# V loads on ScalarE's DMA queue instead of SyncE's, in a one-token attention and SwiGLU kernel

## The chip, the cores and the metric

The kernel runs on one core of one Trainium2 chip. The metric is the device time of one execution in microseconds (us). A core has TensorE (PE in the profile; PEld are its weight loads), VectorE (DVE), ScalarE (ACT), GpSimd (POOL) and SyncE (SP). Each engine works through its own list of instructions in order; a DMA is issued by an instruction in such a list, and what it moves then goes on without the engine.

## The reference

One decoding step for a batch of 4 sequences, with 32 heads of 192, a window of 2048 positions out of the 8192 in the cache, a model width of 640 and an FFN width of 1536. All inputs are bf16.

```
xn  = layernorm(x)                                    # 4 x 640
q   = (xn @ wq) as 32 heads of 192
k, v = the last 2048 positions of k_cache, v_cache    # per batch and head
p   = softmax(q . k * 192**-0.5)
att = (p . v, heads joined: 6144) @ wo
ffn = (silu(xn @ w1) * (xn @ w3)) @ w2
out = x + att + ffn
```

K and V of the window are 32 heads x 4 sequences x 2048 x 192 x 2 bytes each, 100.7 MB for K and the same for V. The weights add 21.6 MB: wq and wo 7.9 MB each, w1, w3 and w2 2.0 MB each.

## The kernel before, in words

**Tiles.** For each head, K is one tile of 128 partitions x 64 positions x 192 (`kt`, 3 MB, two buffers), and V another (`vt`, 3 MB, three buffers). A partition belongs to one of the 4 sequences and holds 64 successive positions, so a row of a load is 24 KB in one piece. The three tiles of wq at the start use the three V buffers.

**Scores.** A head is cut into four units `u = 4h .. 4h+3`. `mult(u)` (L202) multiplies a quarter of K with the query, which is laid out on all partitions (`qbc`), on VectorE. `adder(u)` (L213) adds the product over the 192 columns down to 32 with six matmuls against the identity. `reduce_quarter(u)` (L221) adds those 32 on VectorE, which gives 16 scores for each partition.

**Softmax.** `chain_lmax` (L225) takes the maximum on each partition, `chain_tr` (L230) transposes it, `chain_gmax` (L235, L238) takes the maximum of each sequence, `chain_bc` (L243 to L249) spreads it back with a matmul and computes the exponential `ex` on ScalarE, and `chain_z` (L257) masks it by sequence.

**Values.** `pv(h)` (L265) multiplies `z` with V in 32 matmuls and ScalarE copies the result to `o_raw` (L268). `ge_tot`, `ge_norm` (L280), `ge_tr` (L290) and `ge_copy` (L299) transpose and normalise it. After every four heads `ge_proj` (L194, L195) multiplies with a piece of wo and adds to two accumulators in PSUM, which hold the sum of x, attention and FFN until the end.

**FFN.** Its parts are spread between the heads: w1 is loaded at head 6, w3 after it and w2 last, all in one buffer, so each load waits until the weight before it has been used.

**What sets the order.** There is no automatic scheduler. `add(slot, phase, function, ...)` enters each step in a table, and at the end the table is run through by slot, then phase, then order of entry; each engine gets its instructions in that order. Unit `u` has its product in slot `u`; head `h` has its first unit in `u0 = 4h` and its last in `ul = 4h + 3`. Head h's other steps stand some slots later.

**DMA queues.** All loads but x are issued by SyncE, in slot order:

```
add((h - KBUFS + 1) * GQ, 0, load_k, h)
add(u0 + (2 if h != H - 3 else 5), 0, load_v, h, 1 if h < H - 1 else 2)
```

K of head h is thus issued behind the last product of head h-2, which frees its buffer; V of head h is issued behind K of head h+1. V of head 29 stands at `u0 + 5`, three slots later than the others. The last V is loaded in two pieces. wo for a group of four heads, w1, w3 and w2 stand between them. In a program without a wait SyncE would run ahead of all: what holds it are the waits for buffers.

Of the kernel before, what the change touches and what calls it, by code (L numbers as in the profile page):

```python
# [10 lines left out]
FP32 = mybir.dt.float32  # L11
BF16 = mybir.dt.bfloat16
# [6 lines left out]
def kernel(  # L19
# [14 lines left out]
    KBUFS: int = 2,  # L34
    VBUFS: int = 3,
    PBUFS: int = 4,
    L: int = 8,
    FFN_HEAD: int = 6,
):
    nc = tc.nc  # L40
    P = 128
    B, Sq, D = A_x.shape
    _, H, Sk, Dh = A_k_cache.shape
# [3 lines left out]
    FC = F // P  # L47
    PB = P // B
    NJ = W // PB
    GQ = 4  # L50
# [7 lines left out]
    RPP = QW // P  # L58
    NU = H * GQ
# [4 lines left out]
    assert D % P == 0 and F % QC == 0 and P % B == 0 and W % (PB * GQ) == 0  # L64
    assert JQ * DD == 512 and JQ % 2 == 0 and 2 * Dh <= 512 and 0 < N1 <= 512
    assert (H * Dh) % QC == 0 and NQ % 6 == 0 and QW % P == 0 and Dh % RPP == 0 and P == HG * CT
    assert 2 * H * Dh <= NJ * Dh and KBUFS == 2 and VBUFS == 3

    ctx.enter_context(tc.manual_schedule())
    const = ctx.enter_context(tc.tile_pool(name="const", bufs=1))  # L70
    fpool = ctx.enter_context(tc.tile_pool(name="ffn", bufs=1))
# [4 lines left out]
    small = ctx.enter_context(tc.tile_pool(name="small", bufs=3))  # L76
# [9 lines left out]
    kts, vts, prs, pss, scs, exs, zs = {}, {}, {}, {}, {}, {}, {}  # L86
    wos, o_raws, rsums, rtbs, chs, ges, oTs = {}, {}, {}, {}, {}, {}, {}
# [7 lines left out]
    def load_v(h, pieces=1):  # L95
        vt = vpool.tile([P, NJ, Dh], BF16, tag="vt")
        src = v_win[:, h].rearrange("b (p j) d -> p b j d", p=PB)
        n = NJ // pieces
        for i in range(pieces):
            nc.sync.dma_start(out=vt[:, i * n:(i + 1) * n, :].rearrange("q j d -> q (j d)"),  # L100
                              in_=src[:, :, i * n:(i + 1) * n, :].rearrange("p b j d -> p b (j d)"))
        vts[h] = vt

# [3 lines left out]
        wos[hg] = wo_t  # L107

    x_sb = const.tile([B, D], BF16, name="x_sb")
    nc.scalar.dma_start(out=x_sb[:], in_=A_x.rearrange("b s d -> (b s) d"))  # L110
    wq_v = A_wq.rearrange("(p kc) n -> p kc n", kc=KC)
    wq_rows = []
    for k0 in range(0, KC, 2):
        n = min(2, KC - k0)
        wt = vpool.tile([P, 2, H * Dh], BF16, tag="vt")
        nc.sync.dma_start(out=wt[:, 0:n, :].rearrange("p k n -> p (k n)"),
                          in_=wq_v[:, k0:k0 + n, :].rearrange("p k n -> p (k n)"))
# [49 lines left out]
    for c0 in range(0, NQ, 6):  # L167
        qps = [pool.tile([P, QC], FP32, tag=tag, name="qps")
               for pool, tag in ((ps_add, "ps"), (ps_add, "ps"), (ps_o, "o_ps"), (ps_o, "o_ps"), (ps_m, "mt"), (ps_t, "t"))]
        for kc in range(KC):  # L170
            for i, qp in enumerate(qps):
                nc.tensor.matmul(qp[:], lhsT=xnT[:, kc].rearrange("p a b -> p (a b)"),  # L172
                                 rhs=wq_rows[kc][:, (c0 + i) * QC:(c0 + i + 1) * QC],
                                 start=(kc == 0), stop=(kc == KC - 1))
# [8 lines left out]
    o_banks = []  # L183
    for i in range(2):
        o_ps = ps_o.tile([P, 2 * Dh], FP32, tag="o_ps", name="o_ps")
# [7 lines left out]
    def acc_add(lhsT, rhs, first=False, last=False):  # L193
        nc.tensor.matmul(acc0[:], lhsT=lhsT, rhs=rhs[:, 0:N0], start=first, stop=last)  # L194
        nc.tensor.matmul(acc1[:], lhsT=lhsT, rhs=rhs[:, N0:D], start=first, stop=last)  # L195
# [62 lines left out]
                                in1=mask_b[:].unsqueeze(1).to_broadcast([P, NJ, B]), op=ALU.mult)  # L258
        zs[h] = z

    def pv(h):
        o_ps, z, vt = o_banks[h % 2], zs.pop(h), vts.pop(h)
        for jj in range(NJ // 2):
            c = jj % 4
            nc.tensor.matmul(o_ps[c * CT:c * CT + 2 * B, :], lhsT=z[:, 2 * jj:2 * jj + 2, :],  # L265
                             rhs=vt[:, 2 * jj:2 * jj + 2, :], start=(jj < 4), stop=(jj >= NJ // 2 - 4))
        o_raw = small.tile([P, 2, Dh], FP32, tag="o_raw", bufs=2, name="o_raw")
        nc.scalar.copy(out=o_raw[:].rearrange("q two d -> q (two d)"), in_=o_ps[:])  # L268
        o_raws[h] = o_raw


    def ge_tot(h):
# [35 lines left out]
    hT = const.tile([P, FC, B], BF16, name="hT")  # L308
    g_bf = const.tile([B, F], BF16, name="g_bf")
    ffn = {}  # L310
# [29 lines left out]

    w2_v = B_w2.rearrange("(p c) n -> p c n", c=FC)

    W2C = [(0, FC // 2), (FC // 2, FC - 2), (FC - 2, FC)]

    def w2_load(i):
        if i == 0:
            ffn["w2"] = fpool.tile([P, FC, D], BF16, tag="w", name="w2")
        c0, c1 = W2C[i]
        nc.sync.dma_start(out=ffn["w2"][:, c0:c1, :].rearrange("p c n -> p (c n)"),
                          in_=w2_v[:, c0:c1, :].rearrange("p c n -> p (c n)"))  # L350

    def ffn_out(i):
        for c in range(*W2C[i]):
            acc_add(hT[:, c, :], ffn["w2"][:, c, :], last=(c == FC - 1))

    sched = defaultdict(list)

    def add(slot, phase, fn, *args):
        sched[slot].append((phase, len(sched[slot]), fn, args))


    for h in range(H):
        u0, ul = h * GQ, h * GQ + GQ - 1
        last = h >= H - 2
        if h >= KBUFS:
            add((h - KBUFS + 1) * GQ, 0, load_k, h)
        add(u0 + (2 if h != H - 3 else 5), 0, load_v, h, 1 if h < H - 1 else 2)
        for u in range(u0, ul + 1):
            add(u, 1, mult, u)
            add(u + 1, 2, adder, u)  # L370
            add(u + 1, 8, reduce_quarter, u)
        add(ul + 1, 9, chain_lmax, h)
        add(ul + 2, 3, chain_tr, h)
        add(ul + 2, 4, chain_gmax, h)
        add(ul + 3, 3, chain_bc, h)
        add(ul + 3, 4, chain_z, h)
        add(ul + 4, 5, ge_tot, h)
        add(ul + 4, 9, ge_norm, h)
        add(u0 + L, 7, pv, h)
        add(u0 + L + (1 if h != H - 2 else 3), 7, ge_tr, h)  # L380
        add(u0 + L + (2 if h != H - 2 else 3), 9, ge_copy, h)
    for hg in range(NG):
        a = ((hg + 1) * HG - 1) * GQ + L + 3
        add(hg * HG * GQ + 8 if hg < NG - 1 else NU, 0, wo_load, hg)
        add(a, 6, ge_proj, hg, 0, RPP // 2)
        add(a + 1, 6, ge_proj, hg, RPP // 2, RPP)
    f = FFN_HEAD * GQ
    add(f, 0, ffn_load, "w1", B_w1)
    add(f + 7, 7, ffn_in, "w1", g_bf)
    add(f + 7, 7, ffn_silu)  # L390
    add(f + 7, 9, ffn_load, "w3", B_w3)
    add(f + 15, 7, ffn_up)
    add(f + 15, 8, ffn_h)
    add(f + 16, 7, ffn_transpose)
    add((H - 1) * GQ + 1, 0, w2_load, 0)
    add(NU, 0, w2_load, 1)
    add(NU, 0, w2_load, 2)
    add(NU + L - 5, 8, ffn_out, 0)
    add(NU + L + 2, 0, ffn_out, 1)
    add(NU + L + 2, 0, ffn_out, 2)  # L400

    for s in sorted(sched):
        for phase, _, fn, args in sorted(sched[s], key=lambda e: (e[0], e[1])):
            fn(*args)

    res = ppool.tile([B, D], BF16, tag="pr", name="res")
    nc.vector.tensor_copy(out=res[:, 0:N0], in_=acc0[:])
    nc.scalar.copy(out=res[:, N0:D], in_=acc1[:])
# [31 lines left out]
```

## Time and profile before

| | |
|---|---|
| time, median of 3 runs | 536.11 us (536.1 to 538.67) |
| the profiled execution, its own time | 536.1 us |
| its span, from first to last instruction | 534.3 us |
| granted clock of TensorE, mean | 0.885 |
| TensorE matmul, busy | 378.0 us (71%) |
| VectorE, busy | 353.5 us (66%) |
| ScalarE, busy | 50.3 us (9%) |
| bytes moved, mean rate | 223.39 MB, 418 GB/s |
| one K load, from issue to landing | 19.2 us (median) |
| one V load, from issue to landing | 26.6 us (median) |
| product of one unit (L202) | 1.75 us |
| reduction of one unit (L221) | 0.68 us |
| six matmuls of an adder (L213) | 1.46 us at full clock, 2.64 us where the clock stood near half |

The profile is of one execution. Its page has the busy time of each engine, the span in 40 equal slices of 13.4 us (with a DMA row: how busy the 16 DMA engines were, in tenths), the DMA queues, and the chain of work that ended last: what each step waited for, followed back from the last instruction. A time to landing runs from the issue to the moment when the last byte has arrived, so it includes the transfers that stand ahead in the queue. Idle time of an engine that isn't on that chain costs nothing.

### The profile page before, as it was taken

To read this page: it belongs to the slowest core of one execution; us is meant where nothing else is said; L and a number is where in the kernel's file an instruction comes from. 1 tells how busy PE (TensorE), PEld (TensorE's weight loads), DVE (VectorE), ACT (ScalarE), POOL (GpSimd) and SP (SyncE) were. 2 spreads that over 40 slices of the span, in tenths; PEclk is the share of its full clock that TensorE was granted. 3 is DMA by queue.
4 is the path that set the end of the run, shared out by engine and by line. 5 is a ranking of instruction groups with operands and counts; after the bars stand their busy time and mean duration, and the time that the engine had idled before them with its cause. 6 is when DMAs were issued, how large, how long until landed. Compare 5 with 4: busy or idle time off the path is not lost.

```text
span 534.3 us, 6753 instructions
## 1 busy us (share of the span) xinstructions
PE 378.0 (71%) x2948; PEld 184.1 (34%) x2949; DVE 353.5 (66%) x471; ACT 50.3 (9%) x150; POOL 1.1 (0%) x8
## 2 busy tenths in 40 slices
PE   2875886886666876678748768777648865587777
PEld 1322332443233343333313333333313433243244
DVE  3169785876356686785857767687756778586660
ACT  2111000000410200000000000000000000010010
POOL 0000000000000000000000000000000000000000
PEclk9879886899967999697978997799987999698798
DMA  8999999999999999999999999999999999999992
GB/s 359 436 436 393 420 437 437 427 430 431 433 434 431 428 438 423 434 434 428 432 433 431 432 429 432 436 424 432 432 434 432 428 429 437 431 432 392 429 398 81
DMA packets 11709, 223.39 MB, mean 418 GB/s; under 512 B 1304, under 2 KB 1312, under 8 KB 2720
## 3 DMA queue, kind: packets, MB, share of 16 engines
q1 hardware_dynamic: 11672, 222.96, 97.6%
q8 instruction: 23, 0.38, 0.3%
q14 instruction: 6, 0.05, 0.0%
q10 hardware_dynamic: 8, 0.01, 0.0%
HBM read 222.96 MB, written 0.01 MB: 417 GB/s over the span
## 4 chain that ended last, share of the span: by engine, by line
DMA 56%; PE 24%; DVE 16%; ACT 3%; issue 1%; SPq 0%
DMA kt<-in_A_k_cache_dram 49%; PE ps L213 12%; DVE pr L202 11%; PE gp L290 5%; DMA vt<-in_A_v_cache_dram 3%; DMA wt<-in_A_wq_dram 3%; DVE sc L221 2%; PE qps L172 2%; PE o_ps L265 2%; ACT ex L249 1%; DVE z L257 1%; PE mt L243 1%; PE gt L322 1%; PE acc_240 L195 1%; PE acc_239 L194 1%
## 5 line engine op out<-in xcount | busy, mean ns | idle before, releaser
L213 PE MATMUL ps<-pr,idb 128*128 128x512 bf16 x768 | 219.1, 429 | 133.7 <-DVE pr L202 133.7
L202 DVE TENSOR_TENSOR pr<-kt,qbc 128x3072 bf16<-128x3072 bf16 x128 | 223.6, 1747 | 91.5 <-DMA kt<-in_A_k_cache_dram 91.0
L213 PEld LDWEIGHTS <-idb 128*128 128x128 bf16 x768 | 76.3, 105 | 226.6 <-issue 173.4
L221 DVE TENSOR_REDUCE sc<-ps 128x16 f32<-128x512 f32 x128 | 87.4, 683 | 3.7 <-PE ps L213 2.3
L265 PE MATMUL o_ps<-vt,z 128*8 128x384 bf16 x1024 | 55.5, 350 | 1.7 <-DMA vt<-in_A_v_cache_dram 1.7
L290 PEld LDWEIGHTS gp<-sel,o_raw 128*32 128x32 f32 x768 | 46.8, 151 | 13.8 <-issue 12.8
L290 PE MATMUL gp<-sel,o_raw 128*32 128x4 f32 x768 | 49.6, 199 | 0.6 <-ACT o_raw L268 0.6
L265 PEld LDWEIGHTS <-z 128*8 128x8 bf16 x1024 | 24.8, 89 | 30.1 <-issue 17.9
L257 DVE TENSOR_TENSOR z<-ex,mask_b 128x256 bf16<-128x256 bf16 x32 | 13.6, 425 | 32.5 <-ACT ex L249 32.5
L268 ACT COPY o_raw<-o_ps 128x384 f32<-128x384 f32 x32 | 15.3, 478 | 196.3 <-PE o_ps L265 196.3
L246 ACT COPY negm<-mt 128x1 f32<-128x1 f32 x32 | 5.1, 159 | 243.4 <-PE mt L243 243.4
L172 PE MATMUL qps<-wt,xnT 128*128 128x512 bf16 x59 | 17.6, 463 | 4.7 <-DMA wt<-in_A_wq_dram 4.6
L243 PEld LDWEIGHTS mt<-ones_ff,gneg 1*128 1x128 f32 x64 | 11.0, 215 | 17.7 <-issue 14.3
L178 DVE CAST qbc<-qps 128x512 bf16<-128x512 f32 x6 | 3.8, 685 | 19.0 <-PE qps L172 19.0
L243 PE MATMUL mt<-ones_ff,gneg 1*128 1x1 f32 x64 | 13.8, 282 | 0.6 <-DVE gneg L238 0.6
L235 DVE TENSOR_REDUCE gmax<-mt 1x4 f32<-1x128 f32 x32 | 8.8, 274 | 7.9 <-PE mt L230 7.9
L194 PE MATMUL acc_239<-wo_t,oT 128*4 128x320 bf16 x48 | 13.4, 298 | 0.7 <-DVE oT L299 0.7
L195 PE MATMUL acc_240<-wo_t,oT 128*4 128x320 bf16 x48 | 13.4, 298 | 0.0
L172 PEld LDWEIGHTS <-xnT 128*128 128x128 bf16 x60 | 6.9, 114 | 14.9 <-issue 9.8
L249 ACT ACTIVATE ex<-sc,negm 128x64 bf16<-128x64 f32 x32 | 11.1, 348 | 1.0
L299 DVE TENSOR_TENSOR oT<-gp,rtb 32x24 bf16<-32x24 f32 x32 | 5.6, 176 | 7.5 <-PE gp L290 7.2
L230 PE MATMUL mt<-idf,lmax 128*1 128x128 f32 x32 | 10.2, 317 | 0.0
(59 smaller groups left out, 96.4 us busy)
## 6 DMA issues: line engine op xcount, KB each, us to landing
kt<-in_A_k_cache_dram SPq DMA_DIRECT2D x32, 3072.0 KB, 19.2
vt<-in_A_v_cache_dram SPq DMA_DIRECT2D x31, 3072.0 KB, 26.6
wo_t<-in_A_wo_dram SPq DMA_DIRECT2D x8, 960.0 KB, 20.6
wt<-in_A_wq_dram SPq DMA_DIRECT2D x2, 3072.0 KB, 9.8
vt<-in_A_v_cache_dram SPq DMA_DIRECT2D x2, 1536.0 KB, 31.0
w_806<-in_B_w_dram SPq DMA_DIRECT2D x1, 1920.0 KB, 23.1
w_1059<-in_B_w_dram SPq DMA_DIRECT2D x1, 1920.0 KB
wt<-in_A_wq_dram SPq DMA_DIRECT2D x1, 1536.0 KB, 19.9
```

What stands on the lines that cost most here:

```text
L172: nc.tensor.matmul(qp[:], lhsT=xnT[:, kc].rearrange("p a b -> p (a b)"), rhs=wq_rows[kc][:, (c0 + i) * QC:(c0 + i + 1) * QC], start=(kc == ...
L194: nc.tensor.matmul(acc0[:], lhsT=lhsT, rhs=rhs[:, 0:N0], start=first, stop=last)
L195: nc.tensor.matmul(acc1[:], lhsT=lhsT, rhs=rhs[:, N0:D], start=first, stop=last)
L202: nc.vector.tensor_tensor(out=pr[:], in0=kts[h][:, g * JQ:(g + 1) * JQ, :], in1=qbc[:, h * Dh:(h + 1) * Dh].unsqueeze(1).to_broadcast([P, ...
L213: nc.tensor.matmul(ps[:], lhsT=idb[:], rhs=pr[:, :, kk * DD:(kk + 1) * DD], start=(kk == 0), stop=(kk == NK - 1))
L221: nc.vector.tensor_reduce(out=scs[h][:, g * JQ:(g + 1) * JQ], in_=pss.pop(u)[:], axis=AX.X, op=ALU.add)
L243: nc.tensor.matmul(mt[:, P:P + 1], lhsT=gneg[:].rearrange("o p b -> o (p b)"), rhs=ones_ff[0:1, 0:1], start=True, stop=True)
L249: nc.scalar.activation(out=ex[:], in_=scs.pop(h)[:], func=ACTF.Exp, bias=negm[:, 0:1], scale=SCALE, accum_out=rsum[:])
L257: nc.vector.tensor_tensor(out=z[:], in0=ex[:].unsqueeze(2).to_broadcast([P, NJ, B]), in1=mask_b[:].unsqueeze(1).to_broadcast([P, NJ, B]), ...
L265: nc.tensor.matmul(o_ps[c * CT:c * CT + 2 * B, :], lhsT=z[:, 2 * jj:2 * jj + 2, :], rhs=vt[:, 2 * jj:2 * jj + 2, :], start=(jj < 4), stop= ...
L268: nc.scalar.copy(out=o_raw[:].rearrange("q two d -> q (two d)"), in_=o_ps[:])
L290: nc.tensor.matmul(gp[sl, i, :], lhsT=o_raw[:, part, i:Dh:RPP], rhs=sel[:, part * B:(part + 1) * B], start=(part == 0), stop=(part == 1))
```

## The change

The change has three parts.

First, the queues: `load_v` issues through ScalarE (`nc.scalar.dma_start`), and x, which was ScalarE's only load, goes to SyncE, ahead of wq. K, wo, w1, w3 and w2 stay on SyncE. Slots of the loads of K, V, wo and w1 are unchanged. In ScalarE's list the load of V(h) stands behind `o_raw` of head h-3 and the exponential of head h-2.

Second, the slots of softmax and values. `pv` is cut into two halves of 16 matmuls, in slots `u0 + 10` and `u0 + 12`. The slots of head h, counted from `u0`:

| step | before | after |
|---|---|---|
| reduction of the last unit | 4 | 5 |
| lmax | 4 | 5 |
| transpose / gmax | 5 / 5 | 6 / 7 |
| spread and exponential / z | 6 / 6 | 8 / 9 |
| pv | 8 | 10 and 12 |
| ge_tr / ge_copy | 9 / 10 | 13 / 14 |

For head 30 the kernel before had ge_tr and ge_copy in slot 11; after, all heads are alike.

Third, w2. Before, its first half was issued ahead of the last V, and used in `ffn_out(0)` ahead of the last head's PV; now the three pieces are issued in one step behind the last wo, and all 24 matmuls with w2 stand at the very end. The steps of w1 and w3 stand one to three slots earlier.

```diff
@@ load_v
-            nc.sync.dma_start(out=vt[:, i * n:(i + 1) * n, :].rearrange("q j d -> q (j d)"),
+            nc.scalar.dma_start(out=vt[:, i * n:(i + 1) * n, :].rearrange("q j d -> q (j d)"),
                               in_=src[:, :, i * n:(i + 1) * n, :].rearrange("p b j d -> p b (j d)"))
@@ x
-    nc.scalar.dma_start(out=x_sb[:], in_=A_x.rearrange("b s d -> (b s) d"))
+    nc.sync.dma_start(out=x_sb[:], in_=A_x.rearrange("b s d -> (b s) d"))
@@ values
-    def pv(h):
-        o_ps, z, vt = o_banks[h % 2], zs.pop(h), vts.pop(h)
-        for jj in range(NJ // 2):
+    def pv(h, half):
+        o_ps, z, vt = o_banks[h % 2], zs[h], vts[h]
+        n = NJ // 4
+        for jj in range(half * n, (half + 1) * n):
             c = jj % 4
             nc.tensor.matmul(o_ps[c * CT:c * CT + 2 * B, :], lhsT=z[:, 2 * jj:2 * jj + 2, :],
-                             rhs=vt[:, 2 * jj:2 * jj + 2, :], start=(jj < 4), stop=(jj >= NJ // 2 - 4))
-        o_raw = small.tile([P, 2, Dh], FP32, tag="o_raw", bufs=2, name="o_raw")
-        nc.scalar.copy(out=o_raw[:].rearrange("q two d -> q (two d)"), in_=o_ps[:])
-        o_raws[h] = o_raw
+                             rhs=vt[:, 2 * jj:2 * jj + 2, :], start=(jj < 4), stop=(jj >= 2 * n - 4))
+        if half == 1:
+            zs.pop(h)
+            vts.pop(h)
+            o_raw = small.tile([P, 2, Dh], FP32, tag="o_raw", bufs=2, name="o_raw")
+            nc.scalar.copy(out=o_raw[:].rearrange("q two d -> q (two d)"), in_=o_ps[:])
+            o_raws[h] = o_raw
@@ w2
-    W2C = [(0, FC // 2), (FC // 2, FC - 2), (FC - 2, FC)]
-    def w2_load(i):
-        if i == 0:
-            ffn["w2"] = fpool.tile([P, FC, D], BF16, tag="w", name="w2")
-        c0, c1 = W2C[i]
-        nc.sync.dma_start(out=ffn["w2"][:, c0:c1, :].rearrange("p c n -> p (c n)"),
-                          in_=w2_v[:, c0:c1, :].rearrange("p c n -> p (c n)"))
-    def ffn_out(i):
-        for c in range(*W2C[i]):
-            acc_add(hT[:, c, :], ffn["w2"][:, c, :], last=(c == FC - 1))
+    def w2_load(pieces):
+        wt = fpool.tile([P, FC, D], BF16, tag="w", name="w2")
+        for c0, c1 in pieces:
+            nc.sync.dma_start(out=wt[:, c0:c1, :].rearrange("p c n -> p (c n)"),
+                              in_=w2_v[:, c0:c1, :].rearrange("p c n -> p (c n)"))
+        ffn["w2"] = wt
@@ slots of head h
-            add(u + 1, 8, reduce_quarter, u)
-        add(ul + 1, 9, chain_lmax, h)
-        add(ul + 2, 3, chain_tr, h)
-        add(ul + 2, 4, chain_gmax, h)
-        add(ul + 3, 3, chain_bc, h)
-        add(ul + 3, 4, chain_z, h)
-        add(ul + 4, 5, ge_tot, h)
-        add(ul + 4, 9, ge_norm, h)
-        add(u0 + L, 7, pv, h)
-        add(u0 + L + (1 if h != H - 2 else 3), 7, ge_tr, h)
-        add(u0 + L + (2 if h != H - 2 else 3), 9, ge_copy, h)
+            add(u + 2, 4, reduce_quarter, u)
+        add(u0 + L, 3, pv, h, 0)          # L is 10, was 8
+        add(u0 + L + 2, 3, pv, h, 1)
+        add(ul + 2, 5, chain_lmax, h)
+        add(ul + 3, 4, chain_tr, h)
+        add(ul + 4, 5, chain_gmax, h)
+        add(ul + 5, 4, chain_bc, h)
+        add(ul + 6, 5, chain_z, h)
+        add(ul + 6, 4, ge_tot, h)
+        add(ul + 6, 6, ge_norm, h)
+        add(u0 + L + 3, 3, ge_tr, h)
+        add(u0 + L + 4, 5, ge_copy, h)
     for hg in range(NG):
-        a = ((hg + 1) * HG - 1) * GQ + L + 3
+        a = ((hg + 1) * HG - 1) * GQ + L + 5
...
-    add(f + 7, 7, ffn_in, "w1", g_bf)
-    add(f + 7, 7, ffn_silu)
-    add(f + 7, 9, ffn_load, "w3", B_w3)
-    add(f + 15, 7, ffn_up)
-    add(f + 15, 8, ffn_h)
-    add(f + 16, 7, ffn_transpose)
-    add((H - 1) * GQ + 1, 0, w2_load, 0)
-    add(NU, 0, w2_load, 1)
-    add(NU, 0, w2_load, 2)
-    add(NU + L - 5, 8, ffn_out, 0)
-    add(NU + L + 2, 0, ffn_out, 1)
-    add(NU + L + 2, 0, ffn_out, 2)
+    add(f + 5, 7, ffn_in, "w1", g_bf)
+    add(f + 6, 7, ffn_silu)
+    add(f + 6, 8, ffn_load, "w3", B_w3)
+    add(f + 12, 7, ffn_up)
+    add(f + 13, 7, ffn_h)
+    add(f + 15, 7, ffn_transpose)
+    add(NU + 2, 1, w2_load, [(0, FC // 2), (FC // 2, FC - 2), (FC - 2, FC)])
...
+    w2 = ffn.pop("w2")
+    for c in range(FC):
+        acc_add(hT[:, c, :], w2[:, c, :], last=(c == FC - 1))
```

More of the change, by code (lines that the diff above doesn't have):

```diff
@@ L36 @@
     PBUFS: int = 4,
-    L: int = 8,
+    L: int = 10,
     FFN_HEAD: int = 6,
@@ L66 @@
     assert (H * Dh) % QC == 0 and NQ % 6 == 0 and QW % P == 0 and Dh % RPP == 0 and P == HG * CT
-    assert 2 * H * Dh <= NJ * Dh and KBUFS == 2 and VBUFS == 3
+    assert 2 * H * Dh <= NJ * Dh and KBUFS == 2 and VBUFS == 3 and L == 10
     ctx.enter_context(tc.manual_schedule())
@@ L363 @@
         u0, ul = h * GQ, h * GQ + GQ - 1
-        last = h >= H - 2
         if h >= KBUFS:
             add((h - KBUFS + 1) * GQ, 0, load_k, h)
-        add(u0 + (2 if h != H - 3 else 5), 0, load_v, h, 1 if h < H - 1 else 2)
+        add(h * GQ + (2 if h != H - 3 else 5), 0, load_v, h, 1 if h < H - 1 else 2)
         for u in range(u0, ul + 1):
@@ L370 @@
             add(u + 1, 2, adder, u)
-            add(u + 1, 8, reduce_quarter, u)
-        add(ul + 1, 9, chain_lmax, h)
-        add(ul + 2, 3, chain_tr, h)
-        add(ul + 2, 4, chain_gmax, h)
-        add(ul + 3, 3, chain_bc, h)
-        add(ul + 3, 4, chain_z, h)
-        add(ul + 4, 5, ge_tot, h)
-        add(ul + 4, 9, ge_norm, h)
-        add(u0 + L, 7, pv, h)
-        add(u0 + L + (1 if h != H - 2 else 3), 7, ge_tr, h)
-        add(u0 + L + (2 if h != H - 2 else 3), 9, ge_copy, h)
+            add(u + 2, 4, reduce_quarter, u)
[10 more added lines that the diff above has]
+        add(u0 + L + 4, 5, ge_copy, h)
     for hg in range(NG):
-        a = ((hg + 1) * HG - 1) * GQ + L + 3
+        a = ((hg + 1) * HG - 1) * GQ + L + 5
         add(hg * HG * GQ + 8 if hg < NG - 1 else NU, 0, wo_load, hg)
-        add(a, 6, ge_proj, hg, 0, RPP // 2)
-        add(a + 1, 6, ge_proj, hg, RPP // 2, RPP)
+        add(a, 3, ge_proj, hg, 0, RPP // 2)
+        add(a + 1, 3, ge_proj, hg, RPP // 2, RPP)
     f = FFN_HEAD * GQ
     add(f, 0, ffn_load, "w1", B_w1)
-    add(f + 7, 7, ffn_in, "w1", g_bf)
-    add(f + 7, 7, ffn_silu)
-    add(f + 7, 9, ffn_load, "w3", B_w3)
-    add(f + 15, 7, ffn_up)
-    add(f + 15, 8, ffn_h)
-    add(f + 16, 7, ffn_transpose)
-    add((H - 1) * GQ + 1, 0, w2_load, 0)
-    add(NU, 0, w2_load, 1)
-    add(NU, 0, w2_load, 2)
-    add(NU + L - 5, 8, ffn_out, 0)
-    add(NU + L + 2, 0, ffn_out, 1)
-    add(NU + L + 2, 0, ffn_out, 2)
+    add(f + 5, 7, ffn_in, "w1", g_bf)
[5 more added lines that the diff above has]
+    add(NU + 2, 1, w2_load, [(0, FC // 2), (FC // 2, FC - 2), (FC - 2, FC)])
     for s in sorted(sched):
```

## The prediction, made before the result was known

> **What bounds the kernel now.** I read the page first: its slices (part 2), its queues (part 3) and the shares of the chain that ended last (part 4).
>
> ```profile
> span 534.3 us, 6753 instructions
> ...
> DMA  8999999999999999999999999999999999999992
> GB/s 359 436 436 393 420 437 437 427 430 431 433 434 431 428 438 423 434 434 428 432 433 431 432 429 432 436 424 432 432 434 432 428 429 437 431 432 392 429 398 81
> ...
> q1 hardware_dynamic: 11672, 222.96, 97.6%
> ...
> DMA 56%; PE 24%; DVE 16%; ACT 3%; issue 1%; SPq 0%
> ```
>
> All 222.96 MB come through one queue (q1, SyncE's), whose packets keep the 16 engines busy 97.6% of the span. The mean of slices 5 to 36 is 431 GB/s, the best slice 438. Nothing that leaves the bytes and the rate alone can gain more than the first slice, the two shallow ones (4 and 37) and the last. The chain in order of time, one head:
>
> ```profile
> 178.72 18.87 DMA kt<-in_A_k_cache_dram
> 197.62 1.77 DVE pr L202
> ...
> 206.10 1.77 DVE pr L202
> 207.89 22.46 DMA kt<-in_A_k_cache_dram
> ```
>
> A K tile lands (call it S, here 197.62), VectorE uses it up by E = 207.87, and at E the buffer is free and the load two heads on is issued. It lands 19 to 22 us later, although 3 MB need far less: over the 18 heads from 197.62 to 473.65 there pass 36 K and V loads and 5 of wo, 118.2 MB in 276.0 us, so **7.35 us for one K or V load**, 2.3 for a wo, 4.6 for w1, w3 or w2. The rest is other loads ahead in the same queue. A head costs 14.7 us of transfer and 10.25 us of VectorE: transfers bind, with some 11 us of queued work left at each E. Then the edges, in windows of 1 us and the timeline:
>
> ```profile
> 42.00:43.00 1.00, 1.00 (x6) 0.39 (x4) 1.00 (x2) 0.00 (x0) 0.00 (x0) 1.00 0.41 123
> 43.00:44.00 1.00, 0.19 (x2) 0.06 (x1) 1.00 (x2) 0.00 (x0) 0.00 (x0) 1.00 1.04 319
> ...
> 483.97 0.54 SPq L91 DMA_DIRECT2D kt<-in_A_k_cache_dram  x1
> 484.60 1.20 SPq L100 DMA_DIRECT2D vt<-in_A_v_cache_dram  x2
> ...
> 488.16 1.76 DVE L202 TENSOR_TENSOR pr<-kt,qbc 128x3072 bf16<-128x3072 bf16 x1 [3.42 <-DMA kt<-in_A_k_cache_dram]
> ...
> 525.69 0.48 ACT L268 COPY o_raw<-o_ps 128x384 f32<-128x384 f32 x1 [5.98 <-PE o_ps L265]
> ...
> 531.51 0.41 ACT L408 CAST res<-acc_240 4x320 bf16<-4x320 f32 x1 [5.34 <-PE acc_240 L195]
> ```
>
> Near 42 us the transfers run dry (last two columns: DMA share and GB/s): K2 was issued at 41.65, and they are full again at about 43.2, so **1.5 us from issue to flow**. Slice 4 (393 for 436) prices this hole at 1.3 us. At the other end K31 is issued at 483.97 (E29), while K30 still has until 488.1 to land: no hole for the engine that is last. K31, V29, V30, V31, wo7 and w2 then need 7.35 x 4 + 2.3 + 4.6 = 36.3 us, 488.1 + 36.3 = 524.4, which is where the windows show the transfers end. Behind it: the last PV, o_raw, then 8.7 us from PV's end (525.63) to 534.3.
>
> **What the skill says.** The Trainium skill, DMA: Bandwidth & Descriptors, section "Issuing engines are not separate DMA queues": loads from SP and ACT run on the same 16 engines, and only issue time is saved. An issue here takes 0.54 us against 7.35 of transfer, so nothing to gain there; that the engines are shared no line of before shows, since ACT issues only the 5 KB of x. The section "Queues, rings and completion order" has each engine alternate between queues that have work, packet by packet. Equal packets (K and V rows are both 24 KB) would then share about half and half. I take that; before does not show it.
>
> **The change, part by part.**
>
> *V on ACT's queue.* 33 triggers, about 0.55 us each (18 us), leave SP and join ACT. SP waited 327 us for VectorE and ACT is 9% busy, waiting 243 us for one matmul (negm), so both are covered: 0. But the trigger of V(h) now stands in ACT's order behind the exponential of head h-2, which stands behind the last adder of head h-1 on TensorE. After E(h-1): adder 1.46, half a PV 0.74, broadcast 0.38, negm and ex 0.7, handovers 0.2: issued 3.5 us after E, flowing 5.0 after. Its buffer wait (PV of h-3) ends earlier, as o_raw of h-3 is ahead of it on ACT; behind it queue o_raw(h-2), negm and ex(h-1), not due for a head.
> K and V now share. In the steady state K(h+1) flows from S(h) at half rate, 14.7 us. E(h) = S(h) + 10.0 (next part), so S(h+1) = E(h) + 4.7, when K(h+2) has been flowing-ready since E(h) + 1.5: SP's ring never empties, with 3.2 us to spare (before: 11). V(h+1) comes at S(h+1) + 0.3, just as V(h) ends. The period is still 14.7: **0 in mid-run**. A wo in SP's ring makes K late and V run out; K then gets everything. Carried through, V has 5 us left at the next landing, 12.3 us of work to cover 11.5: still 0, barely. For w1, V7 is held behind three g_bf copies until w1 is used, about S7 + 14.4; wo1, w1 and K8 (14.3 us) fill just that: 0.
>
> *Softmax chain and PV in more slots.* Same instructions. VectorE from S to E: 4 products 1.75, 3 reductions 0.68, z 0.43, lmax 0.22, rtb and oT 0.18 each: 10.0 for 10.25, as waits on ex and the transpose go. VectorE isn't the bound: 0.
>
> *Start.* x ahead of wq on SP: one issue, 0.55 before wq at 0.74; the chain starts there, so **+0.45** (0 to 0.55). V0 and V1 are both on ACT behind the last qbc cast (30.8), not behind K2: they fill the hole at 42: **-1.3**.
>
> *The end.* V29 stands at its head's slot + 5 in both kernels; before, K30's 4.1 us behind V28 covered that. Now it is on ACT behind ex(28), issued 3.5 us after E29. V28 came at E27 + 5.0 and takes 14.7 at half rate: done at E27 + 19.7, while S29 = E28 + 4.7 = E27 + 19.4. So K30 has the engines alone: S30 = S29 + 7.35, E29 = S29 + 10.0, K31 flows at E29 + 1.5. Nothing is queued anywhere meanwhile: a hole of 10.0 + 1.5 - 7.35 = **+4.1 us** (0 if V28 has 4 us left, 5 at most). Then 36.3 us as before, with V31 last or up to 0.7 ahead of w2's last piece.
> After V31's landing: half a PV 1.0 (0.74 to 1.4: the 32 of a head took 1.47 us late, 2.73 where the clock stood at 0.5), then the 8.7 us of before, then 12 more w2 matmuls (first half, formerly done ahead) at 0.135 apart: 1.6. Together 11.3 behind V31 for 9.9 behind 524.4; less 0.3 for V31 being a little early: **+1.1** (0.3 to 2).
> Sum: -1.3 + 0.45 + 4.1 + 1.1 = +4.4. The profiled execution took 536.1 us (span 534.3), the median is 536.11: **540.5**.
>
> **Rivals.**
> 1. *Two rings fill the gaps of one* (not slower). The windows of before dip at single points in mid-run (333 GB/s at 257). If a second ring raised 431 to 437 GB/s over the 427 us of slices 5 to 36, it saves 5.8: 534.7. For it: the best slices. Against: the queue is already busy 97.6%, and the skill expects no bandwidth. It decides from 1.0% more rate.
> 2. *The spare 3.2 us is not enough.* After each wo (8), or each ffn load, transfers run dry for 1 to 1.6 us until E + 1.5, because V's bytes were taken early. For: 0.8 us of margin is less than my errors, and a slow clock of TensorE (adder 2.64 for 1.46) makes V later. Price up to 8 x 1.2 = 10: 541 to 550, say 546.
> 3. *V28 still has 4 us left at S29*, so that no hole opens ahead of K31: 540.5 - 4.1 = 536.4. It needs V to lag K, against the half-and-half sharing.
> That V stays on SP is no case: the code names ACT's queue.
>
> **Numbers.** Main forecast 0.45, rival 2 0.20: slower. Rival 3 0.15: no change. Rival 1 0.20, of which 0.08 faster (with rival 3 it gives 530.6). Measurement can tell about 0.5% from no change (533.4 to 538.8): faster 0.08, same 0.27, slower 0.65. Range 532.5 to 548: from rival 1 with part of rival 3 to most of rival 2.
>
> **What would show it.** Right: a second queue with about 101 MB (32 V tiles); V's median landing time near 15 to 20 us and K's still near 19; slice 4 near 436 GB/s; a window of 3 to 5 us near zero just before K31's issue, and V29 issued 3 to 5 us after it; PV of head 31 waiting for V31, with all 24 w2 matmuls behind the last projection. Wrong: a mid-run rate off 431 by over 4 GB/s either way; regular empty windows (rival 2); no hole near 487 to 491 us (rival 3); or a chain that ends through VectorE.

## The result, and the profile after

The changed kernel takes **558.7 us** (median of 4 runs, 554.5 to 559.21) against 536.11: slower by 4.0%, ratio 1.0399, 95% interval 1.0334 to 1.0463. The prediction had the side right and the size wrong: 540.5 us, at most 548. The profiled execution took 559.15 us. Runs over 1.5% above the fastest of the same kernel stay out of the ratios and their intervals here; medians and ranges are over all runs.

The page of the changed kernel, its first lines, slices, queues and chain shares:

```profile
span 557.4 us, 6720 instructions
...
DMA  8999999999799999999999999999998999978980
GB/s 353 436 425 433 436 434 423 389 429 425 299 405 433 432 428 435 432 393 425 433 425 407 435 419 441 430 392 430 434 426 344 432 423 440 434 303 341 442 337 2
...
q1 hardware_dynamic: 6928, 122.30, 52.5%
q10 hardware_dynamic: 4752, 100.67, 42.1%
...
DMA 62%; DVE 21%; PE 14%; issue 1%; ACT 0%; SPq 0%; ACTq 0%
```

The second queue is there with its 100.67 MB, and transfers still bind. But the GB/s row, which was even in the kernel before, now has dents: 299 in slice 11, 393, 407, 392 and 344 about every fourth slice, 303 to 341 near the end. A slice is 13.9 us, so four or five of them pass in the time of the four heads that share a wo. Outside the dents the slices stay at 419 to 442, as before: what went is time with nothing to transfer, not speed. The same places in windows of 2 us (last three columns: TensorE clock, DMA share, GB/s):

```profile
148.00:150.00 2.00, 1.34 (x4) 0.33 (x3) 0.00 (x0) 0.58 (x1) 0.00 (x0) 0.50 0.26 111
150.00:152.00 2.00, 2.00 (x6) 0.39 (x5) 0.00 (x0) 0.17 (x1) 0.00 (x0) 0.50 0.00 0
...
426.00:428.00 2.00, 1.30 (x6) 0.48 (x5) 1.95 (x3) 0.00 (x0) 0.00 (x0) 1.00 0.29 123
428.00:430.00 2.00, 1.45 (x10) 0.55 (x13) 1.80 (x4) 0.00 (x0) 0.00 (x0) 1.00 0.60 172
...
500.00:502.00 2.00, 1.54 (x7) 0.59 (x7) 1.96 (x3) 0.00 (x0) 0.00 (x0) 1.00 0.07 29
502.00:504.00 2.00, 0.75 (x5) 0.29 (x4) 1.94 (x5) 0.00 (x0) 0.00 (x0) 1.00 0.39 86
```

Three kinds of hole: at 148 the wait for w1's use; at 426 a head behind a wo; at 500 the one ahead of K31 that the prediction had. In windows of 1 us, those from 100 to 521 us with the engines under 70% busy lose about 15 us (1.8 us in mid-run before); shallower dips help to bring the end of the transfers from about 524.5 to 542.5 us, 18 us later. The other 5 us stand behind that end: 14.9 us for 9.8.

### The profile page after: what moved, and what is told of

It is laid out like the page before. It is cut to its first block, busy times and chain, and to the rows that moved or that the text cites. A ratio compares the mean times of both kernels' runs of the same rounds, so it can differ in the third digit from the quotient of the medians.

```text
span 557.4 us, 6720 instructions
## 1 busy us (share of the span) xinstructions
PE 381.9 (69%) x2948; PEld 175.8 (32%) x2949; DVE 349.4 (63%) x471; ACT 48.3 (9%) x150; POOL 1.1 (0%) x8
## 3 DMA queue, kind: packets, MB, share of 16 engines
q10 hardware_dynamic: 4752, 100.67, 42.1%
## 4 chain that ended last, share of the span: by engine, by line
DMA 62%; DVE 21%; PE 14%; issue 1%; ACT 0%; SPq 0%; ACTq 0%
DMA kt<-in_A_k_cache_dram 50%; DVE pr L202 15%; DMA w_756<-in_B_w_dram 5%; PE ps L213 5%; DMA vt<-in_A_v_cache_dram 4%; PE gp L294 4%; DVE sc L221 4%; DMA wt<-in_A_wq_dram 3%; PE qps L172 2%; PE gt L326 1%; PE acc_239 L194 1%; PE acc_240 L195 1%; DVE rtb L284 0%; PE o_ps L266 0%; DVE oT L303 0%
## 5 line engine op out<-in xcount | busy, mean ns | idle before, releaser
L213 PE MATMUL ps<-pr,idb 128*128 128x512 bf16 x768 | 216.7, 427 | 146.7 <-DVE sc L221 143.4
L213 PEld LDWEIGHTS <-idb 128*128 128x128 bf16 x768 | 77.6, 105 | 241.6 <-issue 184.1
L266 PE MATMUL o_ps<-vt,z 128*8 128x384 bf16 x1024 | 59.5, 358 | 5.8 <-DMA vt<-in_A_v_cache_dram 5.8
L266 PEld LDWEIGHTS <-z 128*8 128x8 bf16 x1024 | 20.5, 88 | 46.0 <-issue 36.9
L284 DVE RECIPROCAL rtb<-mt 32x4 f32<-32x4 f32 x32 | 5.7, 179 | 27.1 <-PE gp L294 26.9
L194 PE MATMUL acc_239<-wo_t,oT 128*4 128x320 bf16 x48 | 14.6, 319 | 0.3 <-DVE oT L303 0.3
L195 PE MATMUL acc_240<-wo_t,oT 128*4 128x320 bf16 x48 | 14.6, 320 | 0.0
L243 PEld LDWEIGHTS mt<-ones_ff,gneg 1*128 1x128 f32 x64 | 9.6, 186 | 10.5 <-issue 9.9
L243 PE MATMUL mt<-ones_ff,gneg 1*128 1x1 f32 x64 | 12.3, 259 | 0.0
L326 PE MATMUL gt<-w_756,xnT 128*4 128x512 bf16 x15 | 6.9, 623 | 4.7 <-DMA w_756<-in_B_w_dram 3.4
## 6 DMA issues: line engine op xcount, KB each, us to landing
kt<-in_A_k_cache_dram SPq DMA_DIRECT2D x32, 3072.0 KB, 21.6
vt<-in_A_v_cache_dram ACTq DMA_DIRECT2D x31, 3072.0 KB, 18.9
```

The source lines that it names most:

```text
L213: nc.tensor.matmul(ps[:], lhsT=idb[:], rhs=pr[:, :, kk * DD:(kk + 1) * DD], start=(kk == 0), stop=(kk == NK - 1))
L243: nc.tensor.matmul(mt[:, P:P + 1], lhsT=gneg[:].rearrange("o p b -> o (p b)"), rhs=ones_ff[0:1, 0:1], start=True, stop=True)
L326: nc.tensor.matmul(gt[:], lhsT=xnT[:, kc, 0, :], rhs=wt[:, kc, n0:n0 + QC], start=(kc == 0), stop=(kc == KC - 1))
```

## The experiments

Three theories. **A**: V takes its share early, K comes late, and when small weights or a late V come, the rings run empty before the next load may be issued (a ring is what one queue still has to move). **B**: the new softmax and PV slots are to blame. **C**: two rings carry fewer bytes per us, whatever the order. As in the prediction, S is the moment when a head's K has landed and E the moment when it is used up. The kernel before, run again beside each experiment, had medians of 535.1 to 536.4 us.

### Which part of the change

**Only the queues changed** (a_queue_only), slots and w2 as before.

```diff
-            nc.sync.dma_start(out=vt[...
+            nc.scalar.dma_start(out=vt[...
-    nc.scalar.dma_start(out=x_sb[:], ...
+    nc.sync.dma_start(out=x_sb[:], ...
```

> The kernel before with V on ACT's queue and x on SP's, slots and w2 untouched. Theory A (sharing: V takes half of the engines early, K lands late, and SP's ring has too little left when w1, a wo or the late V29 come): most of the 22 us, 546 to 554 us, with holes in the transfers near w1, and near K31's issue. Theory B (the longer softmax and PV schedule is to blame): 535 to 538. Theory C (two rings move fewer bytes per us whatever the order): about 545, without empty windows in mid-run.

Measured: 560.2 us (551.1 to 563.9; the two that enter the ratio, 551.1 and 559.0, give 1.033, 1.022 to 1.044). The whole loss is there, with a scatter wider than theory A's range; empty windows stand in mid-run (155 to 160, 305 to 309 us) and ahead of K31 (505 to 510).

**Only slots and w2 changed** (b_slots_w2_only): the same lines turned back in the changed kernel.

> The changed kernel with V back on SP's queue and x on ACT's: the new slots and the late w2 alone. Theory A: 537 to 541, no hole in mid-run, the longer tail behind the last V kept. Theory B: 553 to 559. Theory C: 537 to 541.

Measured: **533.2 us** (532.4 to 534.6, ratio 0.9940, 0.9916 to 0.9964), faster than both kernels, and below the 537 to 541 of theories A and C: the late w2 did not cost what was expected. Its page shows what the queue alone decides:

```profile
GB/s 356 443 424 435 418 441 428 437 430 426 437 431 428 437 427 435 424 435 432 433 428 435 427 424 438 435 428 429 432 429 441 427 427 433 433 432 396 437 392 157
...
q1 hardware_dynamic: 11672, 222.96, 98.1%
```

No slice between the third and the 36th is under 418. Theory B is out: the queues are the whole loss and the other two parts a gain of 0.6%.

**Only w2 late** (c_w2_late_only): the three pieces behind the last wo, all 24 matmuls at the end.

```diff
-    add((H - 1) * GQ + 1, 0, w2_load, 0)
...
-    add(NU + L - 5, 8, ffn_out, 0)
...
+    add(NU + 2, 1, w2_load, [(0, FC // 2), (FC // 2, FC - 2), (FC - 2, FC)])
```

> The kernel before with w2 loaded behind the last wo and its 24 matmuls at the very end, all else untouched. If the tail costs what I predicted: +1.6 us for 12 more matmuls at 0.135 apart, 537 to 538. If TensorE stays at half clock in the tail, as in the changed kernel's trace (0.267 apart): +4 to +6, 540 to 542.

Measured: 536.5 us (ratio 1.0003, 0.9970 to 1.0035): no change, below both expected ranges. On one queue w2 is the last to land, so PV of head 31 runs beside its transfer (PV from 520.2 to 522.8 us, the transfers end near 524).

**V29 at slot + 2** (d_v29_early), two queues.

```diff
-        add(h * GQ + (2 if h != H - 3 else 5), 0, load_v, h, 1 if h < H - 1 else 2)
+        add(h * GQ + 2, 0, load_v, h, 1 if h < H - 1 else 2)
```

> The changed kernel with V29 at its head's slot + 2, as the other V loads have it, instead of + 5. If the hole of 3.8 us ahead of K31 (499 to 504 us) comes from V29's late issue: it goes, and the time falls by 3 to 4.5 us, to 554 to 556. If the hole only moves on to the next wait: within 1.5 us of the changed kernel.

Measured: 556.3 us (550.4 to 560.1; 550.4 and 553.4 enter the ratio). The runs scatter too widely to tell a gain of 2.4 us from nothing: inconclusive in time. Its trace does show that the late V29 made the hole: ahead of K31 (issued at 505.7) the windows of 1 us near empty are gone, and two dips at 491 and 493 us lose 1.2 us where the changed kernel loses 3.8.

### Is it the order, or two rings as such?

**VectorE and TensorE relieved**, with two queues (e_half_two) and with one (f_half_one). Scores over half of K's columns only; all bytes still loaded.

```diff
-        nc.vector.tensor_tensor(out=pr[:], in0=kts[h][:, g * JQ:(g + 1) * JQ, :],
+        nc.vector.tensor_tensor(out=pr[:, :, 0:Dh // 2], in0=kts[h][:, g * JQ:(g + 1) * JQ, 0:Dh // 2],
...
-        for kk in range(NK):
+        for kk in range(NK // 2):
```

> The changed kernel (two queues) with the scores taken over only 96 of the 192 columns of K: product 0.88 us for 1.75 and three matmuls for six. All bytes are loaded as before; only VectorE and TensorE are relieved. Theory A (a landed K is used up too late for the next loads to be issued before the rings run dry): E comes 3.5 us sooner after S, spare 3 us rises to 6 or 7, mid-run holes go, 534 to 541 us. Theory C (two rings carry less): the rate in mid-run stays 2 to 3% under that of one queue, 546 or more.

> The same relief (scores over 96 of 192 columns) with V on SP's queue: the one-queue partner. One queue is already bound by bytes, so both theories expect 530 to 533, as without the relief. The gap to the two-queue partner is what counts: under 6 us by theory A, 12 or more by theory C.

Measured: 553.2 us (549.7 to 554.7) with two queues, 532.7 (531.3 to 533.3) with one. This missed theory A's range, and the time and the gap of 20.5 us fell where theory C was expected: E came 7 to 8 us behind S, and still 20 us were lost. So "K is used up too slowly" is not the core of it. But the undented slices of the two-queue page still run at 423 to 437 GB/s, which is not theory C's lower rate. The loss is again in holes, one of them at 298 to 300 us, in the head behind a wo.

**Every V a head earlier** (g_v_ahead), on the kernel before with the two queues.

```diff
-        add(u0 + (2 if h != H - 3 else 5), 0, load_v, h, 1 if h < H - 1 else 2)
+        add(u0 - 2, 0, load_v, h, 1 if h < H - 1 else 2)
```

> The kernel before with V on ACT's queue and x on SP's (slots as before), and every V load placed at its head's slot - 2 instead of + 2 (V29 too): on ACT it stands behind o_raw of head h-3, not h-2, so it is issued a head earlier, as soon as its buffer is free. Theory A: ACT's ring then holds up to 7 us more at each E, the mid-run holes go, 534 to 540. Theory C: 545 or more. If what hurts is that K gets only half of the engines: no better than with V at + 2 (551 to 564).

Measured: 564.5 us (557.6 to 566.0): no help. My reasoning was wrong, and why is instructive: a V is issued when a V buffer comes free, once a head, and is moved at once. V14 is issued 3.0 us behind E12, where the changed kernel issues it 3.7 us behind E13: a head earlier, but still once a head and just behind an E. It then waits longer in SBUF; ACT's ring isn't fuller.

What did the rings do behind a wo? The queue view of the changed kernel, from 268 to 272 us (packets, MB, share of the engines), with V on q10 and on q1 mostly a wo, which most engines have begun although the last bytes of K15 land only at 271.89; and from 288 to 292 us with K and V:

```profile
DMA packets 103, 1.66 MB, mean 415 GB/s; under 512 B 9, under 2 KB 9, under 8 KB 47
...
q10 hardware_dynamic: 53, 1.30, 76.3%
q1 hardware_dynamic: 49, 0.34, 20.3%
...
DMA packets 75, 1.72 MB, mean 430 GB/s; under 512 B 5, under 2 KB 5, under 8 KB 5
...
q1 hardware_dynamic: 39, 0.93, 54.2%
q10 hardware_dynamic: 36, 0.79, 45.7%
```

Packet for packet the rings are even: 49 and 53, 39 and 36. In bytes they are not: a wo's packet is a row of 7.7 KB, V's is 24 KB, so the wo got a fifth of the bytes and held up the K behind it, while V ran ahead. The Trainium skill, DMA: Bandwidth & Descriptors, "Queues, rings and completion order", says turns by packet, and these two windows agree. In single us from 288 to 292 one even sees the turns of the 16 engines: V has 12, 4, 15 and 5 packets, K 4, 14, 3 and 18, so they change after each row of 24 KB. This gave two tests of theory A in a new form: **small weights must not stand in K's ring**, and **packet size sets who gets more of the bytes**.

### Weights out of K's ring

All weights but wq on ACT's queue (i_weights_act), only wo (m_wo_act), only w1, w3 and w2 (n_ffn_act).

```diff
-        nc.sync.dma_start(out=wo_t[:], ...                  # i and m
+        nc.scalar.dma_start(out=wo_t[:], ...
-        nc.sync.dma_start(out=wt[:].rearrange(...           # w1, w3: i and n
+        nc.scalar.dma_start(out=wt[:].rearrange(...
-            nc.sync.dma_start(out=wt[:, c0:c1, :]...        # w2: i and n
+            nc.scalar.dma_start(out=wt[:, c0:c1, :]...
```

> The changed kernel with wo, w1, w3 and w2 on ACT's queue as well, so that SP's ring carries K (and x, wq) alone. In windows of the changed kernel's trace the two rings move equal numbers of packets, so a wo (rows of 7.7 KB) in K's ring gets a quarter of the bytes beside V (24 KB), and K waits behind it. Theory A, in this form (K held up behind small packets while V runs ahead until its buffers are full): holes after each wo go, 540 to 549 us; the hole ahead of K31 may stay. If it is two rings as such: 554 to 560.

> The changed kernel with only wo on ACT's queue; w1, w3 and w2 stay on SP's. If the eight wo loads in K's ring are what costs: most of the 20 us come back, 540 to 546 us, while the hole near w1 (148 to 152 us) stays. If it is the FFN's weights: 552 to 558.

> The complement: only w1, w3 and w2 on ACT's queue, wo stays in K's ring. If wo is what costs: 550 to 556, holes every fourth head kept. If it is the FFN's weights: 540 to 546.

Measured: **538.5** (534.4 to 543.3), **544.4** (544.3 to 545.3) and **553.3** (551.3 to 555.9) us. Against 558.7 that is 20.2 us for all (1.5 us better than expected), 14.3 for wo and 5.4 for the FFN's weights: the parts add up. With only wo moved the dents of every fourth head are gone, and those near w1 and ahead of K31 stay, as the row shows:

```profile
GB/s 348 435 435 432 421 432 433 432 426 438 353 395 432 429 427 433 433 432 424 436 431 434 431 433 427 434 430 429 433 431 429 433 429 434 428 405 339 431 387 13
```

And behind a wo the shares are now the other way round, from 256 to 260 us in the kernel with all weights moved:

```profile
q1 hardware_dynamic: 50, 1.23, 71.2%
q10 hardware_dynamic: 59, 0.42, 25.1%
```

K (q1) has three quarters of the bytes while the wo is in V's ring; V, which has buffers to spare, is the one that waits. The move also changes when a wo is issued: in ACT's list it follows the V of head 13 at once (234.90 behind 234.32), while in SP's list it came 9.9 us behind that V (253.76). No run separates the two.

### Packet size as priority

Every V in four pieces (j_v_four), in two (l_v_two), and four pieces on one queue as the price of the pieces (k_one_v_four).

```diff
-        add(h * GQ + (2 if h != H - 3 else 5), 0, load_v, h, 1 if h < H - 1 else 2)
+        add(h * GQ + (2 if h != H - 3 else 5), 0, load_v, h, 4)       # j, k; 2 in l
```

> The changed kernel with every V loaded in four pieces, rows of 6 KB for 24: still two queues. If the rings take turns by packet, K (24 KB) gets four fifths of the bytes while both have work, as if it had priority, and V fills the rest. Theory A: V no longer runs ahead, K lands in time, 533 to 542 us. If two rings as such cost the time, or the pieces cost more than they give: 553 or more.

> The changed kernel with every V in two pieces, rows of 12 KB: K gets two thirds beside V. Theory A: between one piece (558.7) and four pieces, 538 to 550. If two rings as such cost the time: 553 or more.

> The price of the four pieces by themselves: one queue (V back on SP, x on ACT), new slots, late w2, each V in four pieces. 532 to 537 if smaller rows cost nothing that shows; the same kernel with V whole took 533.2.

Measured: 543.1 (542.7 to 543.7), 541.6 (540.7 to 542.6) and 537.7 us (536.7 to 540.1). Both two-queue kernels gain 16 to 17 us with the weights still in K's ring. K is what gets faster: its median time from issue to landing, on the pages of the changed kernel, of two pieces and of four:

```profile
kt<-in_A_k_cache_dram SPq DMA_DIRECT2D x32, 3072.0 KB, 21.6
...
kt<-in_A_k_cache_dram SPq DMA_DIRECT2D x32, 3072.0 KB, 16.6
...
kt<-in_A_k_cache_dram SPq DMA_DIRECT2D x32, 3072.0 KB, 14.7
```

Four pieces gave no more than two, and were 1 us above the range; the pieces themselves cost 4.5 us on one queue (537.7 for 533.2), which my expectation put at up to 4. The queue view of the kernel with two pieces, from 274 to 278 us:

```profile
q1 hardware_dynamic: 47, 1.16, 67.0%
q10 hardware_dynamic: 50, 0.54, 32.5%
```

Again even in packets, 47 and 50, and K has two thirds of the bytes. Theory C is out as the main cause: two rings with K favoured lose 5 to 8 us against one queue with the same slots (543.1 for 537.7, 541.6 and 538.5 for 533.2), not 25. What these last us are stays open.

### What two queues still cost, and the best version

**All weights on ACT's queue, and two more holes taken away** (o_weights_act_fixed): V29 at slot + 2, w3 used three slots later.

```diff
-    add(f + 12, 7, ffn_up)
+    add(f + 15, 7, ffn_up)
```

> All weights on ACT's queue, and the two holes that this kernel's trace still shows taken away: V29 at slot + 2 (hole of 2 to 4 us ahead of K31) and w3 used three slots later (hole of 4 us near 180). If these two are all that two queues still cost against one (538.5 against 533.2): 531 to 535. If something else remains: 536 or more.

Measured: 539.1 us (533.8 to 541.5, ratio 1.0033, 1.0006 to 1.0060), so something else remains. The profiled execution, the fastest of the 20 at 533.8, has no hole in mid-run; the median is no better than with the holes. What the slower executions lose, no profile here shows: open.

**One queue with V29 at slot + 2** (h_one_v29).

> One queue, new slots, late w2, and V29 at slot + 2: fills the shallow dip at 482 to 484 us that one queue shows too (0.8 us). Against the one-queue kernel with V29 at + 5 (533.2): 532 to 533, a gain of at most 1 us.

Measured: 535.7 us (534.2 to 537.2), 2.5 us worse than at + 5 where a gain was expected. V29 then stands ahead of K31 in the one queue: K31's first product waited for it until 502.2 us, while at + 5 it ran at 498.7 without a wait. The late slot that looked like an oversight is what lets K31 pass.

The best version is thus the changed kernel with V back on SP's queue: 533.2 us.

## Why the prediction failed, point by point

- **What binds, and the price of a load**: right. Transfers bind before and after, and undented slices run at the same rate. The rival of two rings that gain bandwidth is refuted.
- **V issued 3.5 us after E**: right. E15 at 281.73, its V at 285.28; after E10 to E27 it took 3.6 to 5.9 us, mostly 3.7.
- **The signs it named**: V's median time to landing is 18.9 us, inside the 15 to 20; K's is 21.6 where about 19 was expected; regular empty windows, its sign for rival 2, are there.
- **Half and half**: right for K beside V (0.93 and 0.79 MB above), wrong in bytes beside small rows (0.34 and 1.30 MB). The prediction named the packet as the unit and checked that K's and V's rows are equal, but carried wo and w1 through as bytes in line. This belongs to the step that failed, which is the next one.
- **"A wo in SP's ring ... still 0, barely"**: this is the step that failed. The runs put the eight wo at 14.3 us. The sum had 12.3 us of work to cover 11.5, with V at 5 and K at 7.35. In the head after K24 (landed at 416.43), V24 had 2.36 MB to go, 5.5 us at 431 GB/s, as predicted. K25 had only 2.2 of its 3.1 MB, 5.1 us, because engines that end a load early start on the next. And E came 11.35 later, not 10.0, so 10.6 us of work had to cover 12.9. A hole of 2.4 us followed.
- **E = S + 10.0** recurs as an error: 12 of the 30 heads from 2 on took over 11 us, with the adder at half clock (2.72 us) and `rtb` waiting behind `gp` for up to 1.6 us. The trace of before had it too: there 14 of these heads took over 11 us, up to 14.6. The prediction read one head, 10.25, and its 11 us of queued work hid the rest. But a late E alone is not the cause: with E at 7 to 8 us (e_half_two) the holes stayed. Rival 2 had the mechanism of V's bytes taken early, at 0.20 and half the price, but not the packet sizes.
- **w1: "fill just that: 0"**: the chain of the changed kernel shows what it cost:

```profile
115.28 28.17 DMA w_756<-in_B_w_dram
143.59 2.31 PE gt L326 x5
145.92 0.58 ACT g_bf L328
146.54 2.31 PE gt L326 x5
148.87 0.58 ACT g_bf L328
149.50 2.30 PE gt L326 x5
151.82 0.33 SPq L318
```

  TensorE waited for w1 until 143.6 and then ran at half clock: 8.2 us for what took 4.9 in before's trace. Both w3 and V7 wait for its end (V7 behind `g_bf` on ACT, issued at S7 + 17.0 where the prediction had 14.4). K9 waits too, which the prediction left out: its buffer came free at E7, 144.65, but it stands behind w3 in SyncE's list and was issued at 152.25. K8 alone couldn't cover that: 4 us. The FFN's weights together cost 5.4.
- **The hole ahead of K31**: predicted 4.1, measured 3.8 (499 to 504 us).
- **Softmax in more slots at 0**: on one queue, with w2, it brings 2.9 us (0.6%).
- **The start, -1.3 by V0 and V1 on ACT**: slice 4 is at 433, as predicted, but the reason isn't shown. The slots alone, on one queue, bring it to 435, the queue alone to 428, and c_w2_late_only, which changes nothing at the start, to 417. Before's 393 is partly that one execution.
- **The tail**: predicted 11.3 us behind V31, measured 14.3 (543.1 to 557.4). TensorE stood at half clock from 532 to 552 us, so most of the 36 matmuls behind `oT` came 0.267 us apart instead of 0.135, and the half PV took 1.48 us for 1.0. The steps were right, and only the clock was mis-sized.

Not settled: how much of wo's 14.3 us comes from its small rows, how much from standing in K's ring at all, and how much from the moment of its issue (the moves change all three at once; the pieces of V, the rows alone, brought 17 us with the weights in place). Open too is what sets the scatter: among two-queue kernels i_weights_act, o_weights_act_fixed and a_queue_only range over 8 to 13 us, j_v_four, l_v_two and m_wo_act over 1 to 2; the kernel before, on one queue, ranges over 6 to 8.

## What to carry to other kernels

One queue is also an order: here it served the load that was needed first, and kept later ones waiting where they could still fill a gap. On two queues the streams of this kernel shared packet by packet, so V, with more buffers, took its bytes early and the double-buffered K came late, later still where short rows stood in its ring. If you must split, try first to leave the critical stream alone in its ring, price every other load in that ring by packets as well as by bytes, and take the time from landing to use from many heads, not from one.

## What I had not expected of the hardware

Two rings moved about the same number of packets even where the sizes differ by a factor of three (49, all but two of 7.7 KB or less, beside 53 of V), so row length worked as priority here: V in rows of 12 KB instead of 24 took 17 us off the time (541.6 for 558.7). And engines don't end a load together: on one queue a K load counted as landed 3 to 5 us after some engines had gone idle (windows of before: 246 GB/s from 483 to 485 us, K30 landed at 488.1).
